# A linear attention followed by a wide MLP on one core: weight decoding with one vector instruction for a block, and batch 0's queries in two portions

## The chip, the cores and the metric

The kernel runs on one core of a Trainium2 chip. A core has five engines with queues of their own: PE (TensorE, matmuls, with a separate weight load, PEld), DVE (VectorE), ACT (ScalarE), POOL (GpSimd) and SP (SyncE, which here only issues DMA transfers). The metric is the device time of one execution in microseconds (us), as the median of the runs of a kernel.

## The reference

Eight batches of eight heads with 576 tokens of 64 values go through an attention with exponential features; its 4608 rows of 512 go through a two-layer MLP.

```python
proj = np.einsum('bhsd,df->bhsf', x, w_phi)            # 64 -> 128
proj = proj - np.max(np.abs(proj), axis=-1, keepdims=True)
phi  = np.concatenate([np.exp(proj), np.exp(-proj)], axis=-1)
kv  = np.einsum('bhsf,bhsd->bhfd', k_p, v)
z   = np.sum(k_p, axis=2)
num = np.einsum('bhsf,bhfd->bhsd', q_p, kv)
den = np.einsum('bhsf,bhf->bhs', q_p, z)[..., None] + 1e-06
x = (num / den)                                        # -> [4608, 512]
h = x @ w_in                                           # 512 -> 2048
g = h * (1.0 / (1.0 + np.exp(-1.702 * h)))
out = g @ w_out                                        # 2048 -> 512
```

q, k, v and w_phi are float32. The two MLP matrices w_in and w_out arrive as float64.

## The kernel before, in words

**Order of the work.** All instructions are first recorded by a `Recorder` and then emitted by one line, 346, so every row of the profile carries L346. `schedule()` is a list scheduler. It keeps a modelled clock for each engine (`cost`, and `_READY` for the time from one engine to another) and, of the instructions whose inputs are there, takes the one that can start first; among equals the one with the lower due value. Due values come from `R.part(v0, v1, first)`: what is recorded after it is spread from v0 to v1, and on the engines listed in `first` it goes ahead of everything without that mark. The order found so is fixed: each engine runs its queue in it and waits where a semaphore says so.

**Attention.** A unit is one batch and two heads (`attn_unit`): the projection and features of k, the sums kv and z, then the projection and features of q, numerators and denominators (`numden` or `products`, with `across` turning 66-row results into token rows, nf), the quotient xf, and its transposition into x16, split into two float16 parts xh and xl, which the MLP reads. Of the 576 tokens 512 are handled by unit and 64 for all heads of a batch at once (tl, `attn_tail`). The first six units (`NEX`), all of batch 0 and half of batch 1, are "exact": their projection is a float32 matmul (`project_whole`) of values that PE has transposed with float32 instructions. Later units split their inputs into float16 parts and are transposed by DMA. A product of two split values is three matmuls, high by high, high by low, low by high; in batch 0 both parts are stored as float32r, a four-byte type.

**Weights.** `load_weights` is called for j = 0 to 15 in two parts of eight; each call brings block 2j of w_in and block 2j+1 of w_out, 128 x 512 values each, 32 blocks in all. Part 0 is due from -9.8 and part 1 from -7.1 (`WV`), beside the attention of batch 0 and the start of batch 1. A float64 block lands as pairs of 32-bit words, hi and lo, in later slots of the buffer wbuf or in one of the buffers x that are not yet used by attention. It is decoded to float32 by four instructions: POOL makes y, hi times 2^-112; ACT turns the low word into an int; DVE shifts y by three bits and ORs the low part in; DVE ANDs the sign out of hi and ORs it in. The result lies one slot behind the block's float16 parts (`wbuf[:, i + 1]`). Then four matmuls with a stationary matrix `pick` (9 columns, of which one holds ones) sum the magnitudes in the upper halves of the raw values, by row of w_in and for w_out; they read bfloat16 at a step of eight bytes. When a part is complete, `weight_scales` makes two powers of two from the sums, and `split_weights` turns each block into two float16 parts w16 in place, the high one by ACT and the low one by DVE, one block behind another because block i's parts overwrite the slot in which block i-1's float32 values were.

**MLP.** `moe_chunk` works on 256 or 384 tokens. For each j: 12 matmuls into hb for each batch it touches, tanh by ACT (th), g by DVE, its high part gh by ACT and low part gl by DVE, then three matmuls of 512 columns into ab for each 128 tokens. The first 512 tokens are done for part 0 and part 1 of the weights apart, in chunks at 0 and 256, so that they start while part 1 is being decoded. MLP work has the mark `first` on DVE and ACT; so had the splits.

```python
WV = ((-9.8, 0.3, -7.2), (-7.1, 0.2, -5.4))
for i, j in enumerate(js):
    R.part(v0 + dv * i, v0 + dv * (i + 1))
    load_weights(j, wsum, j == js[0], j == js[-1])
R.part(v1, v1)
weight_scales(part_, wsum)
R.part(v1, v1 + 0.1, ("vector", "scalar"))
```

## Time and profile before

| what | us |
|---|---|
| median of 3 runs | 1096.73 (1096.34 to 1098.07) |
| the profiled execution | 1097.82 |
| its span | 1096.0 |
| PE busy | 1062.2 (97%) |
| DVE busy | 857.8 (78%) |
| ACT busy | 712.2 (65%) |
| POOL busy | 242.4 (22%) |

The span begins with the first and ends with the last instruction that the profile shows; the profiled execution's time has 1.8 us more around it. Rows of instruction groups read: line, engine, operation, output<-inputs by tile name, partitions x elements and type, xcount | busy us, mean ns of one | idle time of the engine just before them, with what ended it. A row of windows: start and end, length, busy us and count of each engine, the granted clock of PE as a share of full speed, the DMA share and rate. A timeline row: start, length, engine and operation. In tile names, hb and ab are the two kinds of PSUM banks of MLP and early attention, at the banks of attention, wbuf and x the buffers in which weights are decoded, sw the weights' scales, xf the quotient, g the activation before its split.

### The profile page before, as it was taken

Reading aid. Unit: us, or ns where it says so; the run is one execution under the profiler, and the core shown is the slowest. Engines: PE = TensorE matmul, PEld = TensorE weight load, DVE = VectorE, ACT = ScalarE, POOL = GpSimd, SP = SyncE. Lnnn points to the kernel's source line nnn. Section 1 sums busy time; section 2 is a strip of 40 time slices with the busy share of each in tenths; the row PEclk is TensorE's granted clock in tenths of the full one; section 3 lists DMA queues with packets and bytes.
Section 4 is the critical chain, followed back from the end, with each engine's and each line's share of the span. In section 5 each row is a group of like instructions: output and inputs, shape, how many; then the busy total and the mean of one; then the engine's idle time right before and its main releaser. Section 6 shows DMA issues by size and latency. Waiting matters only on the chain.

```text
span 1096.0 us, 22834 instructions
## 1 busy us (share of the span) xinstructions
PE 1062.2 (97%) x8915; PEld 733.2 (67%) x8915; DVE 857.8 (78%) x1775; ACT 712.2 (65%) x1483; POOL 242.4 (22%) x310
## 2 busy tenths in 40 slices
PE   5997999999999999999999999999999999999997
PEld 3664677778766666678766666677876666577653
DVE  5889988999989997897789987897779877422322
ACT  4576687977677776676777677685677666432423
POOL 6546201322121212221132221121123111100000
PEclk9998999999999999999999999999999999999999
DMA  8854233454243431442243433333223220000101
GB/s 273 277 185 130 76 92 84 79 107 98 61 93 92 96 89 36 81 107 57 32 102 88 109 88 55 64 97 60 49 68 68 39 59 10 11 30 1 30 1 29
DMA packets 174252, 87.80 MB, mean 80 GB/s; under 512 B 140224, under 2 KB 164928, under 8 KB 173888
## 3 DMA queue, kind: packets, MB, share of 16 engines
q1 hardware_dynamic: 174144, 86.34, 33.0%
q8 instruction: 70, 1.15, 0.5%
q14 instruction: 38, 0.31, 0.1%
HBM read 54.59 MB, written 9.44 MB: 58 GB/s over the span
## 4 chain that ended last, share of the span: by engine, by line
PE 78%; DVE 10%; ACT 4%; issue 3%; DMA 2%; POOL 1%; SPq 1%; ACTq 0%; DVEq 0%; POOLq 0%
PE ab L346 31%; PE hb L346 29%; PE at L346 19%; DMA xT<-xs 1%; DVE sm L346 1%; DVE gl L346 1%; ACT e L346 1%; DVE ks L346 1%; DVE g L346 1%; DVE t L346 1%; ACT eh L346 1%; SPq L346 1%; DVE el L346 1%; DVE elb L346 1%; DMA tl<-in_v_dram 1%
## 5 line engine op out<-in xcount | busy, mean ns | idle before, releaser
L346 PE MATMUL hb<-x,wbuf 128*128 128x192 f16 (+3 forms) x3264 | 474.9, 280 | 1.1 <-DVE g L346 1.1
L346 PE MATMUL ab<-wbuf,gh 128*128 128x512 f16 x1152 | 335.8, 380 | 0.8 <-ACT gh L346 0.6
L346 PEld LDWEIGHTS <-wbuf 128*128 128x128 f16 x3264 | 279.1, 98 | 78.0 <-issue 0.9
L346 ACT ACTIVATE th<-hb,usc 128x384 f32<-128x384 f32 (+1 forms) x208 | 116.4, 560 | 130.7 <-PE hb L346 125.0
L346 PE MATMUL ab<-wbuf,gl 128*128 128x512 f16 x576 | 192.2, 380 | 1.3 <-DVE gl L346 1.1
L346 DVE SCALAR_TENSOR_TENSOR g<-th,hb 128x384 f32<-128x384 f32 (+1 forms) x208 | 107.6, 517 | 89.8 <-ACT th L346 87.5
L346 PEld LDWEIGHTS <-gh 128*128 128x128 f16 x1152 | 107.3, 98 | 80.4 <-ACT gh L346 2.9
L346 ACT ACTIVATE gh<-g,al 128x384 f16<-128x384 f32 (+1 forms) x176 | 107.6, 611 | 62.7 <-DVE g L346 62.4
L346 DVE SCALAR_TENSOR_TENSOR gl<-g,al,gh 128x384 f16<-128x384 f32 (+1 forms) x176 | 110.9, 630 | 39.2 <-ACT gh L346 32.9
L346 POOL TENSOR_TENSOR xf<-nf,rc 128x512 f32<-128x512 f32 x28 | 32.8, 1171 | 459.4 <-DVE rc L346 395.1
L346 PE MATMUL at<-ph,xT 128*128 128x128 f16 x944 | 108.6, 221 | 0.4 <-ACT x L346 0.4
L346 ACT ACTIVATE e<-at 128x512 f32<-128x512 f32 x144 | 85.6, 602 | 30.3 <-PE at L346 28.5
L346 DVE TENSOR_REDUCE sm<-at 128x4 f32<-128x512 f32 x126 | 86.1, 683 | 21.3 <-PE at L346 21.1
L346 ACT ACTIVATE e<-t 128x512 f32<-128x512 f32 x144 | 89.9, 640 | 9.8 <-DVE t L346 8.6
L346 PEld LDWEIGHTS <-gl 128*128 128x128 f16 x576 | 55.1, 98 | 51.1 <-DVE gl L346 7.2
L346 DVE SCALAR_TENSOR_TENSOR t<-at,ks,sm 128x512 f32<-128x512 f32 x118 | 87.5, 744 | 1.0
L346 DVE TENSOR_TENSOR el<-e,eh 128x512 f16<-128x512 f32 (+1 forms) x106 | 74.7, 704 | 12.7 <-ACT eh L346 11.1
L346 PE MATMUL at<-vs,eh 128*128 128x132 f32 x208 | 80.2, 386 | 0.0
L346 DVE TENSOR_TENSOR elb<-e,eh 128x512 bf16<-128x512 f32 x104 | 74.8, 719 | 6.7 <-ACT eh L346 6.5
L346 PEld LDWEIGHTS <-xT 128*128 128x128 f16 x944 | 70.2, 98 | 14.3 <-issue 1.3
L346 PE MATMUL at<-kzs,eh 128*128 128x132 f32 x216 | 78.2, 375 | 0.0
L346 ACT ACTIVATE eh<-t 128x512 fp32r<-128x512 f32 x105 | 66.4, 648 | 0.3 <-DVE t L346 0.2
(205 smaller groups left out, 1896.4 us busy)
## 6 DMA issues: line engine op xcount, KB each, us to landing
vn<-in_v_dram SPq DMA_DIRECT2D x64, 128.0 KB, 2.9
kq<-in_k_dram SPq DMA_DIRECT2D x32, 256.0 KB, 3.2
kq<-in_q_dram SPq DMA_DIRECT2D x32, 256.0 KB, 3.0
tl<-in_v_dram SPq DMA_DIRECT2D x18, 384.0 KB, 3.2
x<-in_moe_w_in_dram SPq DMA_DIRECT2D x10, 512.0 KB, 5.3
x<-in_moe_w_out_dram SPq DMA_DIRECT2D x10, 512.0 KB, 4.8
out_dram<-osb SPq DMA_DIRECT2D x38, 128.0 KB, 2.4
out_dram<-osb SPq DMA_DIRECT2D x16, 256.0 KB, 2.5
```

The lines of the kernel that those rows point to most:

```text
L346: f(*[g(a) for a in o.args], **{k: g(a) for k, a in o.kw.items()})
```

## The change

Decoding: the low word is converted by ACT as before; y is made by ACT for even blocks and by POOL for odd ones; POOL compares hi with zero for every block and writes the sign, as -2^15 or 0 in an int16, into the upper half of the converted low word, where its 16-bit half is free; one DVE instruction shifts y and ORs the low word with the sign in. Decoded blocks lie two slots behind their float16 parts (`OFF`), and wbuf has one slot more. The sums of magnitudes by `pick` are replaced by matmuls of a block with itself, 128 columns at a time, read as bfloat16 at a step of four bytes from the decoded block; the diagonal holds sums of squares, and `weight_scales` takes the largest entry and halves its exponent. The splits lose their mark `first` and get due values from -6.97 to -6.6 and from -5.4 to -4.9.

Batch 0: the low parts of features and kz are bfloat16 in place of float32r, with bfloat16 copies of the tail's v and of kf made by POOL to go with them. In all exact units the queries go through projection, features, products, quotient and transposition in two portions of 256 tokens; in units 2 and 3 of batch 0 the second portion has a due value of its own (-6.7 and -6.6). kf and nf have two buffers.

```diff
-        kq=2, vn=1, xs=2, xT=2, ks=12, tl=1, t=4, e=2, eh=3, el=2, ekth=1, ektl=1,
-        eqth=1, eqtl=1, xf=1, kzs=1, kf=1, lq=2, nf=1, nt=1, xo=1, x=3, th=2, g=2, gh=2,
+        kq=2, vn=1, xs=2, xT=2, ks=12, tl=1, t=4, e=2, eh=3, ekth=1, eqth=1, xf=1, kzs=1, kf=2, lq=2, nf=2, nt=1, xo=1, x=3, th=2, g=2, gh=2,
...
+    wone = cp.tile([2, 2], F32, name="wone")
+    nc.vector.tensor_scalar(wone[:, 0:1], ident[0:2, 0:1], 16.0, None, ALU.mult)
+    nc.vector.tensor_copy(wone[:, 1:2], ident[0:2, 1:2])
...
-    wbuf = static("wbuf", [P, NBLK + 1, DM], F32)
+    OFF = 2
+    wbuf = static("wbuf", [P, NBLK + OFF, DM], F32)
...
-    def load_weights(j, wsum, first, last):
+    def load_weights(j, wsq, first, last):
...
-                    s0 = NBLK - 7 + 2 * (i % 4)
+                    s0 = NBLK + OFF - 8 + 2 * (i % 4)
...
-                y = wbuf[:, i + 1]
-                R.gpsimd.tensor_scalar(y, hi.bitcast(F32), 2.0**-112, None, ALU.mult)
-                z = lo
-                R.scalar.activation(z, lo.bitcast(U32), AF.Copy, scale=0.9375 * 2.0**-29)
-                R.vector.scalar_tensor_tensor(
-                    z, y.bitcast(I32), 3, z, ALU.logical_shift_left, ALU.bitwise_or
+                y = wbuf[:, i + OFF]
+                R.scalar.activation(lo, lo.bitcast(U32), AF.Copy, scale=0.9375 * 2.0**-29)
+                if i % 2:
+                    R.gpsimd.tensor_scalar(y, hi.bitcast(F32), 2.0**-112, None, ALU.mult)
+                else:
+                    R.scalar.activation(y, hi.bitcast(F32), AF.Copy, scale=2.0**-112)
+                sign = raw.bitcast(I16).rearrange("p (n w) -> p n w", w=4)[:, :, 1]
+                R.gpsimd.tensor_scalar(
+                    sign, hi.bitcast(F32), 0.0, -(2.0**15), ALU.is_lt, ALU.mult
                 )
                 R.vector.scalar_tensor_tensor(
-                    dst.bitcast(I32), hi, -(2**31), z, ALU.bitwise_and, ALU.bitwise_or
+                    y.bitcast(I32), y.bitcast(I32), 3, lo, ALU.logical_shift_left, ALU.bitwise_or
                 )
-                z = raw.bitcast(BF16).rearrange("p (n w) -> p n w", w=4)[:, :, 1]
-            r = NS - 1 if i % 2 else j % (NS - 1)
+            z = wbuf[:, i + OFF].bitcast(BF16).rearrange("p (n w) -> p n w", w=2)[:, :, 1]
             for c in range(NCT):
+                zc = z[:, c * P : (c + 1) * P]
                 R.tensor.matmul(
-                    wsum,
-                    pick[:, NS - 1 - r : 2 * NS - 1 - r],
-                    z[:, c * P : (c + 1) * P],
+                    wsq[:, i % 2],
+                    zc,
+                    zc,
...
-    def weight_scales(k, wsum):
-        m = small(1, "sc")[0:NS]
-        m2 = small(NS, "sc")[0:NS]
-        R.vector.tensor_reduce(m, wsum, AX.X, ALU.max)
-        pow2(m, m)
-        R.vector.tensor_scalar(m2, ident[0:NS, 0:NS], m, None, ALU.mult)
+    def weight_scales(k, wsq):
+        m = small(2, "sc")
+        m1 = small(1, "sc")[0:2]
+        m2 = small(2, "sc")[0:2]
+        R.vector.tensor_reduce(m, wsq, AX.X, ALU.max)
         tp = psa()
-        R.tensor.matmul(tp[:, 0:NS], ones[0:NS], m2, start=True, stop=True)
-        R.vector.tensor_reduce(wg[:, k, 0:1], tp[:, 0 : NS - 1], AX.X, ALU.max)
-        R.vector.tensor_copy(wg[:, k, 1:2], tp[:, NS - 1 : NS])
+        R.tensor.transpose(tp[0:2, 0:P], m, ident)
+        R.vector.tensor_reduce(m1, tp[0:2, 0:P], AX.X, ALU.max)
+        R.vector.tensor_scalar(
+            m1.bitcast(I32), m1.bitcast(I32), 1, 0x7F800000,
+            ALU.logical_shift_right, ALU.bitwise_and,
+        )
+        R.vector.tensor_scalar(m1, m1, 2.0**64, 2.0**-50, ALU.mult, ALU.max)
+        R.vector.tensor_scalar(m2, wone, m1, None, ALU.mult)
+        R.tensor.matmul(tp[:, P : P + 2], ones[0:2], m2, start=True, stop=True)
+        R.vector.tensor_copy(wg[:, k], tp[:, P : P + 2])
...
-            R.scalar.activation(w16[:, i, 0], wbuf[:, i + 1], AF.Copy, scale=sc)
+            R.scalar.activation(w16[:, i, 0], wbuf[:, i + OFF], AF.Copy, scale=sc)
             R.vector.scalar_tensor_tensor(
-                w16[:, i, 1], wbuf[:, i + 1], sc, w16[:, i, 0], ALU.mult, ALU.subtract
+                w16[:, i, 1], wbuf[:, i + OFF], sc, w16[:, i, 0], ALU.mult, ALU.subtract
...
-    def project_whole(n, bank):
+    def project_whole(n, bank, groups=((0, 1), (2, 3))):
         tp = bank()
         x = new("t").rearrange("p a f -> p (a f)")
-        for j in range(4):
+        w = 2 * P * len(groups)
+        for i, j in enumerate(j for g in groups for j in g):
             R.tensor.transpose(
-                tp[:, j * P : (j + 1) * P], n[:, 2 * j : 2 * j + 2], ident, also=(x,)
-            )
-        R.scalar.copy(x, tp)
+                tp[:, i * P : (i + 1) * P], n[:, 2 * j : 2 * j + 2], ident, also=(x,)
+            )
+        R.scalar.copy(x[:, 0:w], tp[:, 0:w])
         ts = []
-        for g in range(2):
+        for g in range(len(groups)):
...
-        if b:
-            return new(nm + "6"), new(nm + "b" if spare == "el" else nm)
-        return new(spare), new(nm)
+        w = "b" if spare == "el" else ""
+        return new(nm + "6") if b else new(spare + w), new(nm + w)
...
+            vtb = new("vtb")
             for a in range(2):
                 r = slice(a * D, a * D + D)
                 R.scalar.copy(vt[r, :, a, 0, 0:D], tl[r, 2])
                 R.vector.tensor_sub(
                     vt[r, :, a, 1, 0:D], tl[r, 2], f32(vt[r, :, a, 0, 0:D])
                 )
-            return ekt, eqt, (vt, vt)
+                R.gpsimd.tensor_copy(vtb[r, :, a, 0:D], tl[r, 2])
+            return ekt, eqt, (vt, vt, vtb)
...
-                        mm.append(
-                            (vt[0 if i else s][:, hp, h, k], ekt[s][i][:, hp],
-                             o[:, s * NF : s * NF + NF])
-                        )
+                        st = vt[2][:, hp, h] if i else vt[s][:, hp, h, k]
+                        mm.append((st, ekt[s][i][:, hp], o[:, s * NF : s * NF + NF]))
...
+            kzl = new("kzb")
+            R.gpsimd.tensor_copy(kzl, kf)
+            kzl = [kzl[:, s] for s in range(2)]
...
+        def quotient(n, t0, nj):
+            rc = small(2 * nj, "rc").rearrange("p (a j) -> p a j", a=2)
+            nd = nf4[:, :, t0 : t0 + nj]
+            R.vector.tensor_scalar(
+                rc, nd[:, :, :, D], EPS, csx if b == 0 else 2.0**-13, ALU.add, ALU.mult
+            )
+            R.vector.reciprocal(rc, rc)
+            xf = new("xf")[:, 0:nj]
+            (R.vector if b == 0 else R.gpsimd).tensor_mul(
+                xf.rearrange("p j a d -> p a j d"),
+                nd[:, :, :, 0:D],
+                rc.unsqueeze(3).broadcast_to([P, 2, nj, D]),
+            )
+            return xf.rearrange("p j a d -> p j (a d)")
+        if exact:
+            for half_ in range(2):
+                if half_ and late:
+                    R.part(*late)
+                    bank = psa
+                (tq,) = project_whole(kq[:, 1], bank, ((half_, half_ + 2),))
+                eq = features_q(b, tq, True)
                 ndt = psa()[0:DV]
-                products(
-                    True, True, [(kf[:, s, h], eqs[h][:, s], ndt) for s in range(2)]
-                )
-                across(ndt, nf[:, 4 * h : 4 * h + 4])
-            elif h == 0:
-                numden([(0, 0), (0, 1), (0, 2)], nf[:, 0:3])
-        if not exact:
+                for h in range(2):
+                    c = slice(256 * h, 256 * h + 256)
+                    products(
+                        True, True, [(kf[:, s, h], eq[:, s, c], ndt[:, c]) for s in range(2)]
+                    )
+                across(ndt, nf4[:, :, 2 * half_ : 2 * half_ + 2])
+                xj = quotient(nf, 2 * half_, 2)
+                tp = psa()[:, 0:256]
+                for j in range(2):
+                    R.tensor.transpose(tp[:, j * P : (j + 1) * P], xj[:, j], ident)
+                c = slice(256 * half_, 256 * half_ + 256)
+                R.scalar.copy(xh[:, hp, c], tp)
+                R.vector.tensor_sub(xl[:, hp, c], tp, xh[:, hp, c])
...
-            attn_unit(b, hp, nat, tail, nt, x16, i < NEX, bank)
+            attn_unit(
+                b, hp, nat, tail, nt, x16, i < NEX, bank,
+                (-6.9 + 0.1 * hp, -6.85 + 0.1 * hp) if b == 0 and hp > 1 else None,
+            )
...
-        R.part(v1, v1 + 0.1, ("vector", "scalar"))
+        weight_scales(part_, wsq)
+        R.part(*(((-6.97,-6.6),(-5.4,-4.9)))[part_])
```

How the rows move, at three places. In them wbuf_169 and wbuf_170 are the weights' buffer, x_111 to x_114 the x buffers with raw blocks, sw the weights' scales. First DVE's queue between part 0's first splits (rows that read wbuf and sw) and its later ones, before:

```order
L346 SCALAR_TENSOR_TENSOR wbuf_169<-wbuf_169,sw_174 128x512
L346 TENSOR_REDUCE sm_126<-ab_66 128x4
L346 SCALAR_TENSOR_TENSOR x_113<-wbuf_169,x_113 128x512
L346 TENSOR_TENSOR t_90<-ab_66,sm_126 128x512
L346 SCALAR_TENSOR_TENSOR wbuf_169<-wbuf_169,sw_174 128x512
L346 SCALAR_TENSOR_TENSOR wbuf_169<-x_113 128x512
L346 SCALAR_TENSOR_TENSOR x_114<-wbuf_169,x_114 128x512
L346 SCALAR_TENSOR_TENSOR wbuf_169<-wbuf_169,sw_174 128x512
L346 SCALAR_TENSOR_TENSOR wbuf_169<-x_114 128x512
L346 SCALAR_TENSOR_TENSOR x_114<-wbuf_169,x_114 128x512
```

and in the changed kernel:

```order
L347 SCALAR_TENSOR_TENSOR wbuf_170<-wbuf_170,sw_172 128x512 x2
L347 SCALAR_TENSOR_TENSOR wbuf_170<-wbuf_170 128x512
L347 SCALAR_TENSOR_TENSOR wbuf_170<-wbuf_170,sw_172 128x512
L347 SCALAR_TENSOR_TENSOR wbuf_170<-wbuf_170,x_111 128x512
L347 SCALAR_TENSOR_TENSOR wbuf_170<-wbuf_170,sw_172 128x512 x2
L347 SCALAR_TENSOR_TENSOR vts_183<-tl_88,iv_177,vt_188 64x4x64 x2
L347 TENSOR_REDUCE sm_124<-at_63 128x4
L347 SCALAR_TENSOR_TENSOR wbuf_170<-wbuf_170,sw_172 128x512 x2
```

Before, two decoding instructions for each block, of which the second reads and writes x, alternate with single splits; now splits come in pairs, with one decoding instruction for a block between them. 

Second, POOL's queue in the stretch in which blocks are decoded from the x buffers, before:

```order
L346 TENSOR_SCALAR wbuf_169<-wbuf_169 128x512 x4
L346 TENSOR_SCALAR wbuf_169<-x_113 128x512 x2
L346 TENSOR_SCALAR wbuf_169<-x_114 128x512 x2
L346 TENSOR_SCALAR wbuf_169<-wbuf_169 128x512 x4
L346 TENSOR_SCALAR wbuf_169<-x_113 128x512 x2
L346 TENSOR_SCALAR wbuf_169<-x_114 128x512 x2
```

and now:

```order
L347 CAST vtb_186<-tl_88 64x4x64 x2
L347 TENSOR_SCALAR wbuf_170<-wbuf_170 128x512 x6
L347 CAST kzb_185<-kf_102 128x264
L347 TENSOR_SCALAR x_111<-x_111 128x512
L347 TENSOR_SCALAR wbuf_170<-x_111 128x512
L347 TENSOR_SCALAR x_111<-x_111 128x512
L347 TENSOR_SCALAR x_112<-x_112 128x512
L347 TENSOR_SCALAR wbuf_170<-x_112 128x512
L347 TENSOR_SCALAR x_112<-x_112 128x512
L347 TENSOR_SCALAR wbuf_170<-wbuf_170 128x512
```

Instructions that write x are signs, those that write wbuf from x are y; of a pair of blocks there are two signs and one y, and the casts for batch 0's copies stand between them. (In the row of six both kinds stand together, since their tiles read alike.)

Third, ACT's queue near part 0's splits, before:

```order
L346 ACTIVATE wbuf_169<-wbuf_169,sw_174 128x512
L346 ACTIVATE x_113<-x_113 128x512
L346 ACTIVATE wbuf_169<-wbuf_169,sw_174 128x512
L346 ACTIVATE x_113<-x_113 128x512
L346 CAST x_112<-at_62 128x512
L346 ACTIVATE wbuf_169<-wbuf_169,sw_174 128x512
L346 ACTIVATE x_114<-x_114 128x512
L346 CAST zt_190<-xf_104 64x4x64 x2
L346 ACTIVATE wbuf_169<-wbuf_169,sw_174 128x512
```

and now, where part 1's blocks are decoded:

```order
L347 ACTIVATE x_111<-x_111 128x512
L347 COPY nf_107<-at_61 128x2x132
L347 ACTIVATE wbuf_170<-x_111 128x512
L347 ACTIVATE x_111<-x_111 128x512
L347 ACTIVATE xs_72<-tl_88,ks_78 128x4x64 x2
L347 CAST x_110<-at_62 128x256
L347 ACTIVATE x_112<-x_112 128x512
L347 ACTIVATE wbuf_170<-x_112 128x512
```

For two blocks ACT had two conversions of the low word (x<-x); it now has a third instruction that makes y (wbuf<-x). The copy to x16 of 128x256 is the first portion of a unit's tokens.

74 lines of the change are left out of this document (30 added, 44 removed).

## The prediction

> **What bounds the kernel now.** I read the page's first part and the clock row first, then the windows, to see which stage has an engine that others wait for.
>
> ```profile
> span 1096.0 us, 22834 instructions
> PE 1062.2 (97%) x8915; PEld 733.2 (67%) x8915; DVE 857.8 (78%) x1775; ACT 712.2 (65%) x1483; POOL 242.4 (22%) x310
> ```
>
> TensorE is busy for 97% of the span, so only 33.8 us of idle PE exist, and only a shorter PE sum or less of that idle time can shorten the run. The windows say where it lies (the columns are length, busy time with instruction count of each engine, granted clock, DMA share and rate):
>
> ```profile
> 0.00:14.60 14.60, 4.15 (x12) 3.04 (x13) 3.00 (x12) 2.96 (x5) 8.80 (x30) 1.00 0.65 190
> 14.60:72.50 57.90, 54.76 (x318) 37.87 (x318) 51.45 (x90) 37.28 (x73) 29.73 (x19) 1.00 0.79 253
> 72.50:115.10 42.60, 34.19 (x215) 22.87 (x214) 39.57 (x74) 30.54 (x61) 25.86 (x19) 0.84 0.59 178
> 115.10:137.00 21.90, 21.90 (x146) 14.44 (x145) 20.26 (x51) 16.16 (x33) 2.35 (x2) 1.00 0.11 34
> 300.00:1096.00 796.00, 784.98 (x6614) 530.92 (x6611) 588.62 (x1204) 500.55 (x1031) 139.63 (x191) 1.00 0.28 60
> ```
>
> From 115.1 us on PE has few gaps: it is busy for 21.90 of 21.90 us, and for 785 of 796 after 300. The first 14.6 us wait for the first loads, which the change does not touch. Between 14.6 and 115.1 DVE is busy for 91.0 of 100.5 us (51.45 + 39.57), PE for 88.95 with many short instructions, and the clock is 0.84 in the second half. The front is DVE's: the first value of the weights' MLP is ready when DVE has come through its queue.
>
> ```profile
> 115.13 0.42 DVE L346 SCALAR_TENSOR_TENSOR g<-th,hb 128x256 f32<-128x256 f32 x1 [0.19 <-ACT th L346]
> 100.30:113.90 13.60, 8.13 (x55) 6.22 (x56) 13.60 (x23) 7.62 (x14) 11.02 (x8) 0.50 0.68 188
> 102.08 1.11 PE L346 MATMUL at<-ident,xf 128*128 128x128 f32 x4 [4.07 <-DVE xf L346]
> ```
>
> The first row is the first g, at 115.13 us. The second shows DVE busy for all 13.6 us before it while PE works 8.13 us at half clock. The third shows PE idle for 4.07 us behind DVE's xf. What DVE does there, by groups between 14.6 and 115.1 us (busy, mean ns | idle before):
>
> ```profile
> L346 DVE SCALAR_TENSOR_TENSOR wbuf<-wbuf 128x512 int32<-128x512 int32 x24 | 16.9, 734 | 2.8 <-POOL wbuf L346 2.3 <-issue 0.5
> L346 DVE SCALAR_TENSOR_TENSOR wbuf<-x 128x512 int32<-128x512 int32 x16 | 13.0, 811 | 0.0
> L346 DVE SCALAR_TENSOR_TENSOR x<-wbuf,x 128x512 int32<-128x512 int32 x16 | 11.3, 719 | 0.0
> L346 DVE SCALAR_TENSOR_TENSOR wbuf<-wbuf,sw 128x512 f16<-128x512 f32 x11 | 9.0, 821 | 0.5 <-ACT wbuf L346 0.4
> L346 DVE TENSOR_TENSOR xf<-nf,rc 128x512 f32<-128x512 f32 x4 | 2.7, 681 | 0.0
> ```
>
> The first three rows are the decoding of weights, two instructions to a block, 41.2 us in 56 of them; the fourth is the splits into float16 parts.
>
> **The change part by part.** (1) DVE. A block's decoding goes from two instructions to one. By the order of the two kernels, 27 decoding instructions instead of 56 stand ahead of the first g. 29 fewer, at the 0.67 us at which they follow each other when nothing holds them up, is −19.4 us. Against it stand five more splits ahead of g (16 for 11) at 0.75, +3.8; the reductions and subtractions of features and the tl reductions, which come earlier, +2.2; the quotients and the subtractions of x in halves of 256 tokens, where two short instructions take the place of a long one, +0.6; more small reciprocals, +1.5; and the scales, +0.3. The sum is −11.0 us.
>
> The 0.67 is a choice: the rows' means are 0.72 to 0.81, which hold delays. The timeline has a free run, and right behind it a held one (start, length; the last row is a step of the chain of waits):
>
> ```profile
> 76.33 2.48 DVE L346 SCALAR_TENSOR_TENSOR wbuf<-wbuf 128x512 int32<-128x512 int32 x4
> 76.72 6.46 POOL L346 TENSOR_SCALAR wbuf<-x 128x512 f32<-128x512 f32 x3 [9.41 <-DMA x<-in_moe_w_in_dram]
> 81.09 1.76 DVE L346 SCALAR_TENSOR_TENSOR wbuf<-wbuf 128x512 int32<-128x512 int32 x2 [2.28 <-POOL wbuf L346]
> 76.72 3.50 POOL wbuf L346
> ```
>
> Four take 2.48 us, 0.62 each. The bounds are 29 × 0.62 and 29 × 0.81, −18.0 and −23.5, so the sum lies between −9.6 and −15.1.
>
> (2) ACT takes what DVE loses in part. It now makes y for each even block, and it is no longer held to a distance of one slot behind DVE. Its rows in the same stretch:
>
> ```profile
> L346 ACT ACTIVATE x<-x 128x512 int32<-128x512 uint32 x16 | 10.7, 679 | 0.0
> L346 ACT ACTIVATE wbuf<-wbuf,sw 128x512 f16<-128x512 f32 x12 | 8.6, 720 | 4.6 <-DVE wbuf L346 4.6
> L346 ACT COPY xs<-at 66x512 f32<-66x512 f32 x12 | 7.0, 582 | 10.7 <-PE at L346 10.7
> ```
>
> 14 of the new y stand ahead of the first tanh, priced like the conversions of the first row with their delays out, 0.65 each: +9.1. Four or five more splits at 0.72 add 3.4; together +12.5 us. ACT's idle time between 14.6 and 115.1 was 32.7 us (100.5 − 37.28 − 30.54), so it holds them; but after the change some 20 us of idle are left in a front that is to be 11 us shorter, that is 9. With so little slack its waits for PE (10.7 us in the third row) will sometimes decide. Taken for nothing they leave 11; if ACT keeps all its waits the front shortens by 0. I take 7 of the 11, nearer to DVE's sum since its rows were the fullest, and note it as the softest step. The four us of the second row that ACT waited for DVE are what the second slot gives back; no new gain is booked for it.
>
> (3) POOL. It loses 14 of 28 y ahead of the first g and gains 27 signs.
>
> ```profile
> L346 POOL TENSOR_SCALAR wbuf<-x 128x512 f32<-128x512 f32 x20 | 34.6, 1740 | 18.4 <-DMA x<-in_moe_w_in_dram 13.9 <-DMA x<-in_moe_w_out_dram 4.2
> L346 POOL TENSOR_SCALAR wbuf<-wbuf 128x512 f32<-128x512 f32 x12 | 19.1, 1604 | 22.5 <-DMA wbuf<-in_moe_w_in_dram 15.5 <-DMA wbuf<-in_moe_w_out_dram 6.9
> ```
>
> No row shows the sign, which compares, multiplies and writes int16. The nearest row is y's own instruction, of the same engine, kind and length, 1.60 to 1.74 us; the upper bound is two of these in one, 3.5, which is also what the first of the three above took. At the mean of both rows, 1.68, POOL has 41 × 1.68 = 69 us before the first g where it had 47. The two rows together, 53.7 us of work and 40.9 of waiting for loads, are a room of 95 us; the waits shrink first, so the signs stay hidden. At 2.4 us a sign POOL has 27 × 2.4 + 14 × 1.68 = 88 us, with 7 left for all waits, and would decide. I take 1.68: the nearest row.
>
> The Trainium skill speaks against this step: SBUF — State Buffer, section "Who interferes with whom", says that DVE and GpSimd share a pair of ports as an exclusive lock, held for a whole instruction by a DVE instruction with two inputs in SBUF or by a GpSimd one that reads SBUF. The trace agrees in part: the first of the three POOL instructions took 3.50 us beside the four DVE ones that read two inputs, but DVE went on at 0.62 each. By the page each added POOL instruction would hold DVE up, or wait for it, for a whole instruction; the third rival is this mechanism, priced from rows.
>
> (4) PE. The sums of magnitudes with the stationary pick go, the squares come, 128 matmuls for 128.
>
> ```profile
> L346 PE MATMUL hb<-wbuf,pick 128*9 128x128 bf16 x32 | 4.6, 290 | 0.0
> 28.29 1.20 PE L346 MATMUL hb<-wbuf,pick 128*9 128x128 bf16 x9
> 25.35 0.28 PE L346 MATMUL at<-ekth,vts 128*66 128x128 f32 x2
> 194.25 0.61 PE L346 MATMUL at<-ph,xT 128*128 128x128 f16 x8
> ```
>
> Nine picks take 1.20 us, so they follow at (1.20 − 0.29)/8 = 113 ns. Their input is strided by eight bytes. The squares read a stride of four bytes; the nearest rows of 128 columns are four-byte ones that follow at 60 ns (0.28 − 0.22) and dense ones at (0.61 − 0.22)/7 = 56. So 128 × 55 = 7.0 us at most leave PE; nothing at least, if the stationary side's stride costs as much. PE waits in the front, so most of that only becomes waiting there: I take −2, and 0 and −7 for the range. The low parts of batch 0 in bfloat16 have the same number of columns and give at most 1 us, inside that range.
>
> (5) Queries in two portions, and splits without priority. The same PE, ACT and DVE work is cut in halves; the extra instructions are in the sums of (1) and (2). For heads 4 to 7 of batch 0 the second half stands behind the first products of the MLP. That removes work from the queue ahead of g, and PE does it later, when it would be dense: the PE work itself is not saved. The second part's splits stand further back, where DVE is also full:
>
> ```profile
> 178.00:300.00 122.00, 121.20 (x1352) 95.41 (x1350) 119.80 (x281) 92.17 (x214) 29.46 (x41) 1.00 0.41 86
> ```
>
> DVE had 2.2 us of 122 free here, but ahead of it the change still leaves DVE about 8.7 us less work up to the twelfth gl, so no stall is booked. DMA queues: the loads are the same and in the same places of SP's queue; slots move by one block; no wait is put ahead of another load. Price nothing, covered by DVE's room; without it, at worst part of the 7.
>
> **Sum.** Profiled execution 1097.82 us (span 1096.0 and 1.8 around it) − 7 − 2 = 1088.8. The median of the runs is 1.1 lower than the profiled one (1096.73), so 1087.7: **1088 us**. Its own range, from 11 + 3 down to 3 + 0 saved: 1082 to 1094.
>
> **Rivals.** (a) The full gain, and no slow clock. The 13.6 us at 0.50 cost at most half of their length, 6.8. They began behind this:
>
> ```profile
> 96.90:100.30 3.40, 0.98 (x8) 1.00 0.65 205
> ```
>
> PE was busy 0.98 of 3.40 us, and then the clock halved. If the shorter DVE queue leaves no such stretch, PE runs its work before g without it: 11 for DVE, 4 for PE's squares, and 3.5 of the 6.8 that DVE's queue had not already hidden, 18.5 in all: 1078. Against it: PE waits more, not less, if ACT is the next to be late. The Trainium skill has the same rule in TensorE: Matmul & The Clock Gate, "Part 1: The HAM clock gate": the clock halves after an idle window of about 3.4 us and comes back after a busy one; the trace agrees with both.
>
> (b) No change. ACT's 12.5 us come to stand where DVE's 11 went, or the splits wait for the scales, which need all of a part's blocks decoded. The front ends where it did, and 1 us of PE's squares is left: about 1096. For it: ACT's waits for PE do not shrink with DVE's queue. Against: 20 us of ACT idle.
>
> (c) Slower: POOL becomes the bound at the decoding of the second part's blocks, since its instruction blocks DVE or is blocked. With 3.5 us for each sign, 27 × 3.5 + 14 × 1.68 = 118 us from 14.6 on put the last sign ahead of g at 133, some 18 us late, of which PE can cover about 4 with attention of batch 1: 1096.7 + 14 = about 1110. It decides from 2.4 us a sign. For it: the 3.50 us above. Against: the other 31 of POOL's 32 average (34.6 + 19.1 − 3.5)/31 = 1.62 us, and their 40.9 us of idle time waited for loads, none for DVE.
>
> **Chances.** Forecast 0.52, (a) 0.20, (b) 0.13, (c) 0.15. The range to hold eight in ten leaves out the outer part of (a) and the outer half of (c): **1075 to 1104**. A change under 0.2% (2.2 us) cannot be told from none here. Faster is the forecast, (a) and a little of (b): 0.74; within 0.2%: 0.11; slower, (c): 0.15.
>
> **What would show it.** Right: the first g near 108 us rather than 115.13; DVE's decoding group with half its count at 0.6 to 0.75 us; POOL's signs at 1.5 to 1.8 us; squares spaced at 55 to 60 ns; PE dense from the first g on. (a): granted clock 1.00 in the window up to the first g. (b): ACT near full between 75 and 115 and DVE waiting for ACT. (c): POOL's group of signs above 2.4 us, and DVE's idle time ending on POOL. The forecast is wrong in its main step if g comes earlier and the end does not: then PE has a new gap behind 115 us, most likely at the splits of the second part.

## The result, and the profile after

The changed kernel is slower: 1107.73 us as the median of its runs (1107.27 to 1108.88), where the kernel before had 1097.4 us beside it, a ratio of 1.009 with a 95% interval of 1.0075 to 1.0104. The third rival was forecast at 1110; the likeliest case was 1088.

The page of the changed kernel, first its span and busy times:

```profile
span 1105.4 us, 22987 instructions
PE 1057.2 (96%) x8965; PEld 735.0 (66%) x8965; DVE 849.7 (77%) x1767; ACT 723.7 (65%) x1511; POOL 298.9 (27%) x335
```

PE's busy time fell by 5.0 us (1062.2 before) and its idle time rose from 33.8 to 48.2 us: 14.4 us of new waiting make 9.4 us of longer span. DVE's work is 8.1 us shorter, POOL's 56.5 us longer. The windows, at the borders used for the kernel before:

```profile
14.60:72.50 57.90, 49.23 (x311) 35.72 (x311) 45.07 (x79) 41.39 (x85) 50.06 (x25) 0.97 0.81 260
72.50:115.10 42.60, 30.02 (x205) 20.85 (x202) 35.77 (x70) 34.50 (x70) 38.83 (x24) 0.91 0.40 119
115.10:137.00 21.90, 17.73 (x128) 13.21 (x128) 16.75 (x27) 13.19 (x26) 21.74 (x11) 0.87 0.56 170
137.00:178.00 41.00, 41.00 (x297) 30.81 (x296) 37.22 (x93) 33.22 (x71) 10.58 (x14) 1.00 0.29 74
```

DVE (third busy column) went from 91.0 to 80.8 us between 14.6 and 115.1, as the sum of the prediction said. POOL (fifth) went from 55.6 to 88.9, and in the next window it is busy for 21.74 of 21.90 us. PE is busy for 5.5 us less in the first window, 4.2 in the second and 4.2 in the third, where it had no idle time before. POOL's groups of weights (whole span; busy, mean ns of one | idle before):

```profile
L347 POOL TENSOR_SCALAR x<-x 128x512 int16<-128x512 f32 x20 | 54.1, 2750 | 3.6 <-ACT x L347 3.5
L347 POOL TENSOR_SCALAR wbuf<-wbuf 128x512 int16<-128x512 f32 x12 | 32.2, 2730 | 10.1 <-ACT wbuf L347 10.1
L347 POOL TENSOR_SCALAR wbuf<-x 128x512 f32<-128x512 f32 x10 | 18.2, 1821 | 0.1
```

The first two are the signs: 86.3 us in 32 instructions. They overlap at their ends by some 0.2 us; started one behind another they follow at 2.51 us in the median of 30. The third is y, as long as before but for one of 4.16 us (see "The port" below). POOL's weights' instructions no longer wait for loads; the signs wait for ACT, into whose converted low word they write (13.6 us in the first two rows), a wait that the prediction did not have. The chain of waits between 60 and 140 us shows what stands on the other side:

```profile
76.44 4.03 POOL wbuf L347 x2
85.41 4.23 POOL wbuf L347 x2
117.02 4.49 POOL x L347 x2
123.57 4.44 POOL x L347 x2
```

56.6% of that chain is POOL's weights, and DVE waits 12.7 us for POOL between 14.6 and 140 us. The timeline of PE (end of a row: idle time and what ended it) and of DVE show how it arrives there:

```profile
113.54 0.61 PE L347 MATMUL ab<-wbuf 128*128 128x128 bf16 x4 [1.64 <-DVE wbuf L347]
136.49 0.40 PE L347 MATMUL ab<-wbuf 128*128 128x128 bf16 x4 [1.79 <-DVE wbuf L347]
85.65 1.02 DVE L347 SCALAR_TENSOR_TENSOR wbuf<-wbuf 128x512 int32<-128x512 int32 x1 [1.05 <-POOL wbuf L347]
124.55 0.40 DVE L347 SCALAR_TENSOR_TENSOR g<-th,hb 128x256 f32<-128x256 f32 x1
```

The squares of a block stand in PE's queue at a fixed place; the sign is late, DVE's one decoding instruction waits for it, the squares wait for DVE, and all that stands behind them on PE waits too (8.4 us between 14.6 and 140 us). The first g comes at 124.55 us, not at 115.13. The last sign begins at 139.26 us and its block is decoded at 142.51, so part 1's splits begin at 152.63 instead of 136.91.

### The profile page after: what moved, and what is told of

The parts are those of the page before. It is cut to its first block, busy times and chain, and to the rows that moved or that the text cites. A ratio compares the mean times of both kernels' runs of the same rounds, so it can differ in the third digit from the quotient of the medians.

```text
span 1105.4 us, 22987 instructions
## 1 busy us (share of the span) xinstructions
PE 1057.2 (96%) x8965; PEld 735.0 (66%) x8965; DVE 849.7 (77%) x1767; ACT 723.7 (65%) x1511; POOL 298.9 (27%) x335
## 4 chain that ended last, share of the span: by engine, by line
PE 73%; DVE 11%; POOL 8%; issue 3%; ACT 2%; DMA 2%; SPq 1%; ACTq 0%; DVEq 0%; POOLq 0%
PE hb L347 29%; PE ab L347 29%; PE at L347 15%; POOL wbuf L347 4%; POOL x L347 3%; DVE sm L347 2%; DVE t L347 1%; DVE wbuf L347 1%; SPq L347 1%; DVE elb L347 1%; DVE gl L347 1%; DVE g L347 1%; DVE ks L347 1%; DVE el L347 1%; DMA xT<-xs 1%
## 5 line engine op out<-in xcount | busy, mean ns | idle before, releaser
L347 PEld LDWEIGHTS <-wbuf 128*128 128x128 f16 (+1 forms) x3392 | 286.0, 98 | 89.6 <-DVE wbuf L347 12.4
L347 POOL TENSOR_TENSOR xf<-nf,rc 128x512 f32<-128x512 f32 (+1 forms) x30 | 32.1, 1069 | 465.0 <-DVE rc L347 389.1
L347 PE MATMUL at<-ph,xT 128*128 128x128 f16 x944 | 111.0, 221 | 1.0 <-DVE nf L347 0.6
L347 DVE TENSOR_TENSOR el<-e,eh 128x512 f16<-128x512 f32 x104 | 73.3, 705 | 16.8 <-ACT eh L347 13.6
L347 DVE TENSOR_TENSOR elb<-e,eh 128x512 bf16<-128x512 f32 x106 | 77.5, 732 | 7.7 <-ACT eh L347 7.5
```

What stands on the lines that cost most here:

```text
L347: f(*[g(a) for a in o.args], **{k: g(a) for k, a in o.kw.items()})
```

## The experiments

All ratios are to runs of the kernel before on the same chip (its median was between 1098.8 and 1099.7 us there, 1097.4 beside the changed kernel); 0.001 is 1.1 us. The names used below: the *signs* are POOL's, *whole* queries are those of one portion, *old due values* are the splits' of the kernel before, with their priority.

### Is it the signs' length?

Short signs: the instruction is planned as before, but covers 8 of 512 columns, and the order of instructions is that of the changed kernel on DVE, ACT, PE and SP.

```diff
+                R.force = 100 + 3.4 * DM        # planned cost, as without the edit
                 R.gpsimd.tensor_scalar(
-                    sign, hi.bitcast(F32), 0.0, -(2.0**15), ALU.is_lt, ALU.mult
+                    sign[:, 0:8], hi.bitcast(F32)[:, 0:8], 0.0, -(2.0**15), ALU.is_lt, ALU.mult
                 )
```

> The changed kernel with its order of instructions untouched on every engine, but each of POOL's 32 sign instructions writes 8 of 512 columns, so most weights lose their sign and the output is not the reference's. Theory 1 (POOL is the bound: a sign follows the last one after 2.51 us, 32 of them with 16 y at 1.55 keep POOL busy without a gap from 23 to 140 us): POOL's room comes back, DVE no longer waits for POOL (12.7 us before) and PE no longer for DVE's decoding behind its squares (8.4 us); 1107.7 - 14 us of added PE idle time = about 1094, down to 1085 if the shorter DVE queue now shows. Theory 2 (the order is the cause: squares in PE's queue, queries in portions, splits without priority): the waits move but stay, 1103 to 1108.

Measured: 0.9981 (0.9969 to 0.9992). That is 1097 us, a little above the first theory's range and well below the second's. From 1.0090 to 0.9981 the signs' length is worth 1.09%, 12 us. So the first theory holds for the loss, but not for the forecast: what is left is 2 us of gain, not 9.

Signs back on DVE:

```diff
-                R.gpsimd.tensor_scalar(sign, hi.bitcast(F32), 0.0, -(2.0**15), ALU.is_lt, ALU.mult)
                 R.vector.scalar_tensor_tensor(
-                    y.bitcast(I32), y.bitcast(I32), 3, lo, ALU.logical_shift_left, ALU.bitwise_or
+                    lo, y.bitcast(I32), 3, lo, ALU.logical_shift_left, ALU.bitwise_or
                 )
+                R.vector.scalar_tensor_tensor(
+                    y.bitcast(I32), hi, -(2**31), lo, ALU.bitwise_and, ALU.bitwise_or
+                )
```

> The changed kernel with the signs back on DVE: two DVE instructions for a block as before, all else as changed. Theory 1: POOL has only 16 y, 25 us, and waits for loads again; DVE has 32 instructions more, at 0.67 us 21 us, some 18 of them ahead of the first g, so the front is about as long as in the kernel before, less PE's 5 us: 1090 to 1098. Theory 2: DVE's queue is longer and the order's waits stay, 1107 or more.

Measured: 1.0027 (1.0016 to 1.0038), 1102: above the range of the first theory and below that of the second. Without POOL's signs the rest of the change makes the kernel slower by 3 us when DVE has its two instructions again.

The planner's constant alone:

```diff
+                R.force = 2510.0
                 R.gpsimd.tensor_scalar(sign, hi.bitcast(F32), 0.0, -(2.0**15), ALU.is_lt, ALU.mult)
+                R.force = None
```

> The changed kernel with one constant of the scheduler changed: a sign is planned at 2510 ns (what the trace shows) in place of 1841. No work is added or removed, only the order moves. Theory 1: POOL still has 32 x 2.51 + 16 x 1.55 = 105 us to do, the last block is decoded as late: 1102 to 1108. Theory 3 (the loss is PE standing behind squares that the order put too early, because it planned signs as too short): the 8.4 us of PE's waits for decoded blocks go, 1097 to 1101.

Measured: 1.0035 (1.0022 to 1.0049), 1103. It falls inside the first theory's range, but the gain of 6 us on the changed kernel is more than that theory explains: the same work in an order that knew the length of the signs loses less. PE's waits for decoded blocks are not gone there, 8.1 us between 14.6 and 140 us; the MLP's products start at 116.3 us instead of 119.7.

Half of the signs on each engine:

```diff
+                if i % 2 == 0:      # POOL's sign and one DVE instruction
+                else:               # two DVE instructions
```

> The changed kernel with signs by POOL for even blocks only (whose y ACT makes) and by a second DVE instruction for odd blocks (whose y POOL makes). POOL then has 16 x 2.51 + 16 x 1.55 = 65 us, DVE 16 x 0.67 = 11 us more than in the changed kernel and 11 less than in the one before. Theory 1: POOL is off the bound and DVE is lighter than before: 1084 to 1094, below the kernel before. Theory 2: 1100 to 1108.

Measured: 0.9988 (0.9978 to 0.9997), 1098, some 11 us below the changed kernel and 1.3 us below the one before, between the ranges of both theories. POOL is off the bound; the forecast's gain is still not there.

### What else took the gain?

Three candidates: ACT, PE's waits behind squares, and the queries' portions with the new due values. To the run with short signs come 32 short conversions on ACT:

```diff
-                R.scalar.activation(lo, lo.bitcast(U32), AF.Copy, scale=0.9375 * 2.0**-29)
+                R.scalar.activation(lo[:, 0:8], lo.bitcast(U32)[:, 0:8], AF.Copy, scale=0.9375 * 2.0**-29)
```

> The run with short signs, order unchanged, and beside it ACT's 32 conversions of the low word write 8 of 512 columns (the weights' low bits are then left out, and low parts are combined by AND to keep values finite; not the reference's output). That takes about 32 x 0.45 = 14 us from ACT, somewhat more than the 16 new y put on it (10.7 us). Theory A (with the signs gone ACT is the next bound: it is busy for 24.5 of 32.5 us and 20.7 of 22.5 us in the stretches 40 to 72.5 and 72.5 to 95 us, and PE's idle time grows by 6 us in the same two): PE's idle time there goes back to that of the kernel before, 1087 to 1091. Theory B (PE stands behind squares in its own queue) and C (the queries' second portions and the order behind 95 us): 1095 to 1098, as with short signs alone.

Measured: 0.996 (0.9945 to 0.9975), 1095, against 0.9981 with short signs alone. The step is 2 us and the intervals overlap: ACT is no main cause. PE's idle time between 40 and 95 us is 7.0 us, against 7.4 with short signs; theory A said it would go.

Squares that read a constant block, with short signs and the same order:

```diff
+                zf = ident.bitcast(BF16).rearrange("p (n w) -> p n w", w=2)[:, :, 1]
+                R.ops[-1].args = (wsq[:, i % 2], zf, zf)
```

> The run with short signs, order unchanged, and the 128 squares read a constant 128x128 block with the same step of four bytes in place of the decoded weights, so that PE never waits for a decoded block (the weights' scales are then not those of the data, which is left out). Theory B: PE's waits for DVE's wbuf, 4.0 us between 14.6 and 140 us in the run with short signs, are gone and the end comes 3 to 4 us earlier, 1092 to 1094. Theories A and C: PE waits for the next thing in its queue instead, 1096 to 1098.

Measured: 0.9953 (0.9937 to 0.997), 1094.5. That is the 3 us that theory B gave, at the edge of what the intervals tell apart.

Everything about the weights as before, with the queries' portions and the due values as changed:

```diff
-    def load_weights(j, wsq, first, last):      # one decoding instruction, POOL's signs, squares
+    def load_weights(j, wsum, first, last):     # two, no signs on POOL, pick
-    OFF = 2
+    OFF = 1
```

> One part of the change alone: weights are loaded, decoded, summed with pick and scaled as in the kernel before (POOL makes y, DVE decodes with two instructions, one slot behind), while batch 0's portions, its bfloat16 low parts and the splits' due values are as changed. Theory C (portions and due values cost by themselves): slower than the kernel before by 3 us or more, 1102 or more beside a kernel before at 1099.3. Theories 1 and A (what was lost came through POOL's signs and ACT's y alone): within 2 us of the kernel before.

Measured: 1.0102 (1.0085 to 1.0119), 1111. POOL has no sign to do here, and the kernel is as slow as the changed one. There is a second cause, as large as the first when it stands alone.

A version that spreads the work:

```diff
+                if not (i % 4 == 0):                 # y on POOL, planned at 1550 ns; else on ACT
+                if i % 4 == 0 or i % 8 == 2:         # sign on POOL, planned at 2520 ns; else on DVE
```

> A version spread over the engines, with all weights exact: y by ACT for 8 of 32 blocks and by POOL for 24, signs by POOL for 12 and by a second DVE instruction for 20; the scheduler plans POOL's two kinds at the measured 1550 and 2520 ns. POOL has 24 x 1.55 + 12 x 2.51 = 67 us, DVE 12 x 0.67 = 8 us less than in the kernel before, ACT 5 us more. If theories 1 and A are the whole loss, neither POOL nor ACT bounds the front and it ends at 1090 to 1095; if C holds, 1097 to 1101.

Measured: 0.9989 (0.9979 to 0.9999), 1098. As with half of the signs, and inside the range given for theory C.

### Which part costs what

Four kernels with one part each put back, or one part alone. In all of them, and in every run here, batch 0's low parts stay bfloat16 and kf and nf keep their two buffers; these were not tried apart. First the weights' part alone:

```diff
-            for half_ in range(2):
...
+            tq = project_whole(kq[:, 1], bank)      # whole queries
-        R.part(*(((-6.97,-6.6),(-5.4,-4.9)))[part_])
+        R.part(v1, v1 + 0.1, ("vector", "scalar"))  # old due values
```

> The weights' part of the change alone (decoding with y on ACT and POOL, signs on POOL, squares, two slots ahead; batch 0's low parts in bfloat16 too): queries whole and splits with their old due values and their priority, as in the kernel before. Theory 1 (POOL's signs cost by themselves): POOL has 105 us to do before the last block is decoded, the end is later than the kernel before by 3 to 10 us. Theory C (the loss is in portions and due values, as the run with the old weights says, 11.5 us): no slower than the kernel before, -6 to +2 us.

Measured: 1.0077 (1.0062 to 1.0092), 1108. The signs' part costs 8.5 us without the portions.

The portions (and the bfloat16 low parts) alone, weights and due values old:

```diff
-        R.part(*(((-6.97,-6.6),(-5.4,-4.9)))[part_])     # on top of the old weights
+        R.part(v1, v1 + 0.1, ("vector", "scalar"))
```

> The portions of queries alone (with the bfloat16 low parts): weights as before, splits with old due values and priority. Theory P (portions cost: twelve more short instructions on DVE in a front that DVE bounds, and second portions late): +5 us or more against the kernel before. Theory D (the splits' due values without priority are what cost): within 3 us of the kernel before.

Measured: 1.0106 (1.0089 to 1.0123), 1111. Theory D, that the due values cost it, falls: with them 1.0102, without 1.0106.

The changed kernel with old due values:

```diff
-        R.part(*(((-6.97,-6.6),(-5.4,-4.9)))[part_])
+        R.part(v1, v1 + 0.1, ("vector", "scalar"))
```

> The changed kernel with only the splits' due values and priority put back. Theory D: the loss of the run with old weights (11.5 us) belongs to the due values, so 1096 to 1101 here. Theory P or theory 1 (signs): 1105 to 1110, as in the changed kernel.

Measured: 1.0109 (1.0094 to 1.0124), 1111. The new due values help by about 2 us, if anything.

The changed kernel with whole queries:

```diff
-            for half_ in range(2):
...
+            tq = project_whole(kq[:, 1], bank)
```

> The changed kernel with only the queries put back to one portion of 512 tokens; the splits' due values stay as changed. Theory P: 1096 to 1101. Theory D or theory 1: 1105 to 1112.

Measured: 1.0048 (1.0033 to 1.0063), 1105. Between both theories: the portions cost the changed kernel 0.42%, 4.6 us. A small part of it is PE work that I had not seen. The page of this run, and behind it that of the portions alone:

```profile
PE 1053.3 (96%) x8917; PEld 726.2 (66%) x8917; DVE 849.1 (77%) x1745; ACT 723.3 (66%) x1499; POOL 297.8 (27%) x333
```

```profile
PE 1065.8 (96%) x8963; PEld 739.1 (67%) x8963; DVE 863.6 (78%) x1799; ACT 716.7 (65%) x1495; POOL 241.6 (22%) x321
```

With portions PE has 48 matmuls more and is busy for 3.9 us more than without (8965 and 1057.2 against 8917 and 1053.3), and for 3.6 us more than the kernel before when they stand alone. Most of that, by the estimate below, is not more work but work at a slower clock. The stretches in which PE's granted clock is 0.50, first with whole queries, then in the changed kernel (of the engines, PE alone is shown):

```profile
98.55:115.62 17.07, 5.61 (x35) 0.50 0.54 160
52.41:55.82 3.41, 2.75 (x7) 0.50 0.44 145
103.61:107.02 3.41, 3.02 (x11) 0.50 0.78 259
110.44:120.68 10.24, 5.39 (x39) 0.50 0.56 152
```

PE is busy there for 5.6 and 11.2 us, and for 8.2 in the kernel before and 12.2 with the portions alone. If this time is counted at half, an estimate, 1.1 of the 3.9 us and 1.6 of the 3.6 us are work. When the portions stand alone, PE's idle time rises by 9.8 us (43.6 of a span of 1109.4 us); that is most of their 12 us. First the window of the kernel before, then that of the run with the portions alone:

```profile
72.50:95.00 22.50, 21.97 (x141) 14.54 (x140) 19.82 (x44) 17.92 (x37) 9.94 (x7) 1.00 0.52 162
```

```profile
72.50:95.00 22.50, 15.36 (x79) 10.76 (x78) 19.63 (x43) 15.21 (x29) 10.47 (x7) 0.77 0.17 53
```

and the timeline of PE in that run:

```profile
83.39 0.66 PE L347 MATMUL at<-ident,xf 128*128 128x128 f32 x2 [4.01 <-DVE xf L347]
86.70 1.11 PE L347 MATMUL at<-ident,t 128*128 128x128 f32 x4 [2.44 <-DVE t L347]
123.44 4.05 PE L347 MATMUL hb<-x,wbuf 128*128 128x256 f16 x22
```

PE, which was busy for 21.97 of 22.5 us between 72.5 and 95 in the kernel before, is busy for 15.36 there, behind a quotient and a feature that DVE reaches late: DVE's first split of part 0 is at 79.64 us, 9 us earlier than before, and between 79.64 and 92 DVE does six splits and ten decoding instructions. The MLP's products start at 123.44 instead of 112.54 us. That DVE's queue lies so is the trace; why the scheduler, given the portions, puts the scales and splits ahead of attention was not tried by itself.

### Do the two losses add?

Half of the signs with whole queries:

```diff
+                if i % 2 == 0:      # POOL's sign; else two DVE instructions
+            tq = project_whole(kq[:, 1], bank)
```

> Signs half on POOL and half on DVE, and queries in one portion (all weights and results exact). Costs that add: the halved signs gave 10 us against the changed kernel, whole queries 4.7 us (1.0090 to 1.0048 of the kernel before), so together 0.9988 - 0.0042 = 0.995 of the kernel before, 1094. Costs that overlap (both only make DVE's and POOL's queue in the front too long, and one remedy is enough): no better than 0.9988.

Measured: 0.9991 (0.9982 to 1.0001), 1098: no better than with portions.

The spread version with whole queries:

```diff
+                if i % 4 == 0 or i % 8 == 2:         # sign on POOL, planned at 2520 ns; else on DVE
+            tq = project_whole(kq[:, 1], bank)
```

> The spread version (y by ACT for 8 blocks, signs by POOL for 12, POOL planned at measured lengths) with queries in one portion. Costs that add: 0.9989 - 0.0042 = 0.995 of the kernel before. Costs that overlap: 0.998 to 1.001.

Measured: 0.998 (0.9971 to 0.999), 1097. One us better than with portions, at the edge of the intervals.

Short signs with whole queries:

```diff
+                    sign[:, 0:8], hi.bitcast(F32)[:, 0:8], 0.0, -(2.0**15), ALU.is_lt, ALU.mult
+            tq = project_whole(kq[:, 1], bank)
```

> Short signs (8 of 512 columns, planned at full length as in the run with short signs; most weights lose their sign, not the reference's output) with queries in one portion. With POOL out of the way and the order that of the run with whole queries: if portions cost 4.7 us whatever POOL does, 0.9981 - 0.0042 = 0.994 of the kernel before; if their cost is only shown where POOL or DVE is late, 0.998 or more. It also gives what the whole decoding part is worth without the signs: the forecast's sum of 9 us would be 0.992.

Measured: 0.9921 (0.9904 to 0.9937), 1090.3. Here is the forecast's size, 9 us below the kernel before: with the signs' length gone, the portions are worth 0.6%, and with the portions gone, the signs' length is worth 1.27%, 14 us. Its page, its second window and its first g:

```profile
span 1087.5 us, 22844 instructions
PE 1051.3 (97%) x8917; PEld 726.5 (67%) x8917; DVE 841.4 (77%) x1745; ACT 721.2 (66%) x1499; POOL 228.4 (21%) x333
```

```profile
14.60:72.50 57.90, 53.01 (x344) 37.10 (x343) 43.81 (x76) 46.38 (x93) 19.78 (x31) 1.00 0.90 285
72.50:115.10 42.60, 33.76 (x248) 23.75 (x247) 40.42 (x77) 36.70 (x74) 22.61 (x26) 0.88 0.49 145
```

```profile
103.87 0.41 DVE L347 SCALAR_TENSOR_TENSOR g<-th,hb 128x256 f32<-128x256 f32 x1
```

The first g is at 103.87 us, 11.3 us earlier, near the DVE sum of 11.0, though that sum was for queries in portions. But PE's idle time is 36.2 us, 2.4 more than before; between 14.6 and 115.1 us it is 13.7, where it was 11.6. The whole gain is PE's busy time, 10.9 us less: the rows of squares are busy for 12.4 us where those of pick were for 18.5, and the stretch at a clock of 0.50 is 10.2 us long where it was 13.7.

The weights' part with signs on DVE, whole queries, old due values:

```diff
+                    y.bitcast(I32), hi, -(2**31), lo, ALU.bitwise_and, ALU.bitwise_or   # DVE, for all blocks
+            tq = project_whole(kq[:, 1], bank)
+        R.part(v1, v1 + 0.1, ("vector", "scalar"))
```

> The weights' part alone with its signs on DVE: two DVE instructions for a block as in the kernel before, y half on ACT, squares in place of pick, two slots ahead; queries whole, splits with old due values. DVE's and POOL's work are then no longer than before, and what is left of the change is PE's squares (7 us of pitch, of which some lies in the front) and the second slot. If the forecast's PE term is right and nothing else moves, 2 to 7 us faster than the kernel before, 0.994 to 0.998; if the squares' wait for the second DVE instruction (pick waited for the first alone) costs PE as much, 0.999 to 1.003.

Measured: 1.001 (1.0 to 1.0019), 1100. What is left of the weights' part when DVE keeps its two instructions (squares, the second slot, half of y on ACT) gives nothing, although PE is busy for 7.2 us less. The windows show where that went: DVE is as full as before, 92.0 of 100.5 us, and PE is idle for 18.6 us where it was for 11.6; 8.4 of them end on DVE, 3.9 of these on decoded blocks.

```profile
14.60:72.50 57.90, 50.04 (x317) 35.63 (x316) 53.46 (x94) 41.33 (x83) 15.46 (x11) 0.97 0.85 275
72.50:115.10 42.60, 31.88 (x214) 21.52 (x212) 38.57 (x74) 35.16 (x71) 18.07 (x16) 0.84 0.45 130
```

### A shorter sign

The wanted bits, 0x8000 or 0, are those of a signed zero in bfloat16. One multiplication by 0.0 makes them; the order stays that of whole queries, and that of the changed kernel in the second run.

```diff
+                zero = raw.bitcast(BF16).rearrange("p (n w) -> p n w", w=4)[:, :, 1]
+                R.gpsimd.tensor_scalar(zero, hi.bitcast(F32), 0.0, None, ALU.mult)
-                R.gpsimd.tensor_scalar(sign, hi.bitcast(F32), 0.0, -(2.0**15), ALU.is_lt, ALU.mult)
```

> The changed kernel with queries in one portion and the sign made another way, order unchanged: POOL multiplies hi by 0.0 and writes the signed zero as bfloat16, whose bits are the wanted 0x8000 or 0, with one operation and no conversion to int16. All results exact. If the sign's length of 2.51 us comes from its second operation or from int16, it takes about 1.55 us as y does; POOL then has 32 x 1.55 + 16 x 1.55 = 74 us and the time lies near the run with short signs and whole queries, 0.992 to 0.996 of the kernel before. If the length stays at 2.5 us, 1.005 as with whole queries.

Measured: 0.9976 (0.9967 to 0.9985), 1096.6 where the kernel before had 1098.8. The time lies between the two cases of the expectation. This is the lowest ratio of the kernels with all of the work, though its interval overlaps with that of the spread version with whole queries, and it beats both the changed kernel and the one before, the latter by 0.2%.

The same sign in the changed kernel itself:

```diff
-            tq = project_whole(kq[:, 1], bank)      # portions again
```

> The changed kernel itself with only the sign made as a signed zero, order unchanged, queries in portions. If the sign's length is what the change lost by and portions cost what they cost with short signs (0.6%), 0.998 to 1.001 of the kernel before; if the sign's length stays, 1.009.

Measured: 1.0039 (1.0024 to 1.0053), 1103.5 us: 0.5% better than the changed kernel. Expected was 0.998 to 1.001 for a sign of 1.55 us; it did not become that short. POOL's groups of the run with whole queries:

```profile
L347 POOL TENSOR_SCALAR x<-x 128x512 bf16<-128x512 f32 x20 | 46.1, 2350 | 1.5 <-ACT x L347 1.4
L347 POOL TENSOR_SCALAR wbuf<-x 128x512 f32<-128x512 f32 x10 | 16.8, 1683 | 0.1
```

The sign follows at 2.09 us in the median, 0.42 less than the one with two operations and int16, and 0.58 more than y with its four-byte output. POOL is still busy for all 22.50 us between 72.5 and 95.

## Why the prediction was wrong, point by point

**The step that failed first is (3): "I take 1.68: the nearest row."** A sign costs 2.51 us. The prediction's own breakpoint was 2.4, so the third rival held in its place (POOL at the second part's blocks) and in its sign (signs above 2.4 us, DVE's idle time ending on POOL). That its price, 1110, lies near 1107.7 is luck: it took 3.5 us for a sign, because POOL and DVE block each other, and nothing for the portions, while a sign is 2.51 us long without DVE beside it and the portions are 4.6 us of the loss. The upper bound, 3.5, was right to be kept. The nearest row had the engine, the kind and the length in common with the sign, but not the two operations, the 16-bit output and its step of eight bytes; with one operation and bfloat16 at that step it takes 2.09, with two and int16 2.51. Part of the harm is done by the plan: the scheduler took a sign for 1.84 us, and with 2.51 in its place 6 of the 10 us come back. The chance of 0.15 for this rival was too low, since the taken value lay only 0.7 us below the breakpoint and the prediction's own upper bound 1.1 us above it.

**(5), the portions at nothing, failed as well.** "The same PE, ACT and DVE work is cut in halves" is not so on PE: 48 matmuls more, 1 to 2 us of work by the estimate above. With the rest they cost 0.32 to 0.63% where the weights' part is the new one (1.0077 to 1.0109, 1.0048 to 1.0090, 0.9921 to 0.9981, 0.9976 to 1.0039 with the zero's sign), little or nothing in the versions with fewer signs on POOL (0.998 to 0.9989, 0.9991 to 0.9988), and 1.06% alone. The losses of signs (0.77% alone) and portions overlap: together 1.09% with old due values, not 1.83%. That both lengthen the same front and PE waits there once is the likely reading; no run shows it by itself.

**(1), DVE's sum of 11 us, was right as a sum**: 10.2 us less work between 14.6 and 115.1 us in the changed kernel, and the first g 11.3 us earlier in the run with short signs and whole queries. The step from there to the end, "I take 7 of the 11", is not borne out: PE's idle time did not fall in that run.

**(4), PE's squares, came out in busy time, not in the step to the end.** Four of them take 0.41 us and one 0.22 in the changed kernel (timeline, and the group between 0 and 160 us):

```profile
33.99 0.41 PE L347 MATMUL hb<-wbuf 128*128 128x128 bf16 x4 [0.18 <-DVE wbuf L347]
L347 PE MATMUL hb<-wbuf 128*128 128x128 bf16 x64 | 6.4, 221 | 3.6 <-DVE wbuf L347 3.6
```

That is (0.41 − 0.22)/3 = 63 ns each, near the forecast's 55 to 60, and 128 × (113 − 63) = 6.4 us, near its upper bound of 7. PE's busy time fell by 6.7 us in the weights' part alone (1062.2 to 1055.5), by 7.2 with signs on DVE and whole queries, and by 10.9 with short signs and whole queries. But of the first two runs one is 8.5 us slower than the kernel before and the other no faster: all of it became waiting there. Only in the third does it reach the end, where −2 was taken. So that run's 9 us are the forecast's number out of other terms, which is luck: nothing from less idle time, for which 7 was taken, and all from PE's busy time. What the squares cost is in the same place: a square waits for the finished block, where pick waited for the first of the two instructions (the one that writes x; the text on the change calls it the second), and with that wait taken away (constant block) the end comes 3 us earlier, at the edge of what the intervals tell apart.

**(2), ACT**, is near full between 72.5 and 95 us in the run with short signs (20.66 of 22.5 us), as the prediction feared, but 14 us less work there gave some 2 us, with intervals that overlap.

**The port.** The row of 3.50 us that spoke for a mutual lock came back once, with a y of 4.16 us that stands in the chain of waits. Its row, and the first and the last of the five DVE instructions beside it:

```profile
128.60 4.16 POOL L347 TENSOR_SCALAR wbuf<-x 128x512 f32<-128x512 f32 x1
128.28 0.67 DVE L347 TENSOR_TENSOR ektl<-e,ekth 128x512 f16<-128x512 f32 x1
130.68 0.67 DVE L347 TENSOR_TENSOR eqtlb<-e,eqth 128x512 bf16<-128x512 f32 x1
```

In both cases DVE ran instructions with two inputs in SBUF (tiles other than hb, ab and at) without a gap, from before POOL's instruction began, and POOL's ended 1.4 us after the last of them. So POOL did stand still for DVE, some 2.0 us before and 2.7 us in the changed kernel; it happened once in each and is not what makes a sign long. The other way round, 12 of DVE's decoding instructions begin and end inside one of POOL's signs in the changed kernel: the eight that begin in its first 0.31 us take 0.91 to 1.16 us, the four that begin later 0.65 to 0.68, as with POOL idle. So DVE does not stand still for a whole sign. The Trainium skill, SBUF — State Buffer, section "Who interferes with whom", has it that whoever issues first gets the shared pair of ports for the whole instruction and the other fully blocks. The trace agrees where POOL came behind a run of DVE's; where DVE came behind a sign of 2.51 us it lost 0.2 to 0.5 us, and there the measurement decides.

**The slow clock.** It did not go in any of these runs: the granted clock is 0.91 between 72.5 and 115.1 and 0.87 in the next window in the changed kernel, 0.88 in the fastest front, and PE has at least 10.2 us at 0.50 in each of them. So the condition of rival (a) never came about.

What stays open: why the scheduler's order with portions holds attention back so much when the weights are decoded as before (9.8 us of idle PE), and which part of the sign's extra 1 us belongs to the type, which to the step of its output and which to the second operation.

## What to carry to other kernels

When work moves to an engine that looks free (POOL was busy for 22% of the span, but for 55.6 of the 100.5 us in question), price the moved instruction from a row with the same number of operations and the same output type and stride, and if there is none, give the breakpoint the chance that the distance to the nearest row deserves: here a factor of 1.5 turned a hidden engine into the bound. Look at what stands behind the moved work in the fixed order of the next engines; a list scheduler that plans an instruction at 1.84 us when it takes 2.51 puts consumers too early, and here correcting that constant alone gave back 6 of 10 us. And an earlier start of a stage is no gain by itself: what counts is whether the busiest engine's work or idle time gets smaller.

## What the runs showed of the hardware

A GpSimd instruction of 128 x 512 elements, read at a step of eight bytes, takes 1.50 us with one operation and a float32 result, 2.09 with one operation and a bfloat16 result at a step of eight bytes, and 2.51 with two operations and int16 at that step; over 8 columns it takes about 0.21. One that began behind a gapless run of VectorE instructions with two inputs in SBUF ended 1.4 us after the run, 3.50 and 4.16 us long instead of 1.50; a VectorE instruction that began within the first 0.31 us of a GpSimd one took 0.91 to 1.16 us instead of 0.68. TensorE takes 63 ns for 128 bfloat16 columns that it reads at a step of four bytes, with a stationary side at the same step, and 113 ns at a step of eight bytes.
